# Attention backward for one query per head: K scores, dq and softmax sums ahead of the V transposes on TensorE, and the V load behind the dv stores

## The chip, the cores and the metric

One core of a Trainium2 chip. The metric is the device time of one execution in microseconds (us), median of several. Executions of one kernel are compared with executions of the kernel before on the same chip in the same rounds.

## The reference

32 heads, one query row, 8192 keys, head size 128, everything bfloat16. The outputs are the attention result and the gradients of q, k and v.

```python
def _fwd_reference(q, k, v):
    scale = q.shape[-1] ** -0.5
    scores = jnp.einsum('bhqd,bhkd->bhqk', q, k) * scale
    attn = _softmax(scores, axis=-1)
    return jnp.einsum('bhqk,bhkd->bhqd', attn, v)
# reference: out, vjp = jax.vjp(_f, q, k, v); returns (out, dq, dk, dv)
```

Each head reads 2 MB of K and 2 MB of V and writes 2 MB of dk and 2 MB of dv: 268 MB in all, for very little arithmetic. dk is the outer product of ds and q, dv that of p and grad_out; ds needs p, the V scores (grad_out times V) and one scalar.

## The kernel before

K is transposed on VectorE (`k_blocks`), V on TensorE with ScalarE copying out (`v_transposes`), so that both can be contracted over the head size. All transfers are issued by SyncE, in program order (in the trace of the kernel before: dk at 311.09 us, K 313.23, dk 314.01, dv 317.78, V 320.21, dv 320.64); it is the order of the Python calls below that each engine follows. There are three K buffers, two V buffers, and two each for dk and dv. `outer` also issues the stores, 1 MB each.

```python
    for h in range(H + 1):
        p_ = h - 1
        if h < H:
            x = st[h] = {}
            for u in range(NCH):
                k_blocks(h, u)              # VectorE, needs K of head h
            v_transposes(h, 0)              # TensorE, needs V of head h
            v_transposes(h, 1)
            k_scores(h)
            v_scores(h, 0)
        if h > 0:
            ds_of(p_)
            outer(p_, "dk", 0)
        ...                                 # mask, swap, first half of dq, dk part, maximum
        if h > 0:
            dq_of(p_, 1)
        if 0 < h and h + 2 < H:
            load_k(h + 2)
        if h > 0:
            outer(p_, "dk", 2)
        ...                                 # exponentials, rows, sum
        v_transposes(h, 2)
        contract(Vt[h], x["p"], x["m"][:, 2:3])      # the p column sums
        nc.scalar.copy(o_all[:, h:h + 1], x["m"][:, 2:3])
        v_scores(h, 2)
        v_transposes(h, 3)
        ...                                 # scalar product of o and grad_out
        v_scores(h, 3)
        outer(h, "dv", 0)
        outer(h, "dv", 1)                   # stores the first half of dv
        if h + 2 < H:
            load_v(h + 2)
        outer(h, "dv", 2)
        outer(h, "dv", 3)                   # stores the second half
```

Of the kernel before, what the change touches and what calls it, by code (L numbers as in the profile page):

```python
# [24 lines left out]
def kernel(  # L25
# [13 lines left out]
    _, H, S, D = k.shape  # L39
# [23 lines left out]
    def rows_of(x, h, c, parts):  # L63
        L = NT // parts
        return x[0, h].rearrange("(p n) d -> p n d", p=P)[:, c * L:(c + 1) * L, :]

    def slots(X, c, parts):
        L = NT // parts
        return X[:, c * L:(c + 1) * L, :]

    def load_k(h):
        Kt[h] = kpool.tile([P, NT, D], BF16, tag="K", name="Kt")
        parts = NCH if h == 0 else 1
        for c in range(parts):
            nc.sync.dma_start(slots(Kt[h], c, parts), rows_of(k, h, c, parts))

    def load_v(h):
        Vt[h] = vpool.tile([P, NT, D], BF16, tag="V", name="Vt")
        parts = NCH if h in (0, H - 1) else 1
        for c in range(parts):  # L80
            nc.sync.dma_start(slots(Vt[h], c, parts), rows_of(v, h, c, parts))
# [46 lines left out]
    def k_blocks(h, u):  # L128


        if u == 0:
            XK[h] = ktpool.tile([P, CH, NB, NCH, QD], F32, tag="XK", name="XK_sb")
        nc.vector.transpose(XK[h][:, :, :, u, :],  # L133
                            slots(Kt[h], u, NCH).rearrange("p g d -> p (g d)").bitcast(F32).rearrange(
                                "p (g w j) -> p g w j", g=CH, w=NB))

    def k_scores(h):
        x = st[h]
        x["s"] = psS.tile([P, 512], F32, tag="s", name="s_ps")
        out = x["s"][:, 0:NT].rearrange("p (a g) -> p g a", a=NQ)  # L140
        cols = XK.pop(h).rearrange("p g w u i -> p (g w u i)").bitcast(BF16).rearrange(
            "p (g w ui e) -> p g w e ui", g=CH, w=NB, e=2)
        for g in range(CH):
            for c in range(2 * NB):
                nc.tensor.matmul(out[:, g, :], lhsT=cols[:, g, c // 2, c % 2], rhs=q_blk[:, h, c, :],  # L145
                                 start=(c == 0), stop=(c == 2 * NB - 1), skip_group_check=True)
# [18 lines left out]
    def v_transposes(h, c):  # L165
        T_ps = psT.tile([P, CH, P], BF16, tag="T", name="T_ps")
        for i in range(CH):
            nc.tensor.transpose(T_ps[:, i, :], Vt[h][:, c * CH + i, :], ident[:])  # L168
        X = tpool.tile([P, CH, P], BF16, tag="XT", name="XT_sb")
        nc.scalar.copy(X.rearrange("p c s -> p (c s)").bitcast(F32),  # L170
                       T_ps.rearrange("p c s -> p (c s)").bitcast(F32))
        XV[h, c] = X

    def v_scores(h, c):
        X = XV.pop((h, c))
        if c == 0:
            st[h]["dp"] = psD.tile([P, 512], F32, tag="dp", name="dp_ps")
        for i in range(CH):
            n = c * CH + i
            nc.tensor.matmul(st[h]["dp"][:, n:n + 1], lhsT=X[:, i, :], rhs=doT[:, h:h + 1],  # L180
                             start=True, stop=True, skip_group_check=True)

    def contract(Xt, rep, out_col, first=0, last=NT):
        for n in range(first, last):
            nc.tensor.matmul(out_col, lhsT=Xt[:, n, :], rhs=rep[:, n, 0:1],  # L185
                             start=(n == 0), stop=(n == NT - 1), skip_group_check=True)

    def outer(h, which, r):
        x = st[h]
        if r == 0:  # L190
            x[which] = gpool.tile([P, NT, D], BF16, tag=which, name="G_" + which)
        G, dst = x[which], out_2 if which == "dk" else out_3
        rep, row = x["ds"] if which == "dk" else x["p"], x["qd"][:, 0 if which == "dk" else 1, :]
        Q = NT // 4
        nc.vector.tensor_tensor(  # L195
            slots(G, r, 4).rearrange("p n (a b) -> p n a b", b=R),
            slots(rep, r, 4).unsqueeze(2).to_broadcast([P, Q, D // R, R]),
            row.rearrange("p (a b) -> p a b", b=R).unsqueeze(1).to_broadcast([P, Q, D // R, R]),
            op=ALU.mult)
        parts = 4 if h == H - 1 else NST  # L200
        if r % (4 // parts) == 4 // parts - 1:
            c = r // (4 // parts)
            nc.sync.dma_start(rows_of(dst, h, c, parts), slots(G, c, parts))

    def rows_bc(h):
        x = st[h]
        nc.tensor.matmul(x["m"][:, 256:512], lhsT=ident[0:H, h:h + 1].to_broadcast([H, P]),  # L207
                         rhs=rows[:].rearrange("h a d -> h (a d)"), start=True, stop=True,
                         skip_group_check=True)
        x["qd"] = small.tile([P, 2, D], BF16, tag="qd", name="qd")  # L210
        nc.scalar.copy(x["qd"][:].rearrange("p a d -> p (a d)"), x["m"][:, 256:512])
# [10 lines left out]
    def dq_of(h, half):  # L222
        out = st[h]["dp"][:, 128:129]
        contract(Kt[h], st[h]["ds"], out, half * NT // 2, (half + 1) * NT // 2)
        if half == 1:
            nc.scalar.copy(dq_all[:, h:h + 1], out)  # L226
# [4 lines that stand above are left out]
            x = st[h] = {}  # L231
            for u in range(NCH):
                k_blocks(h, u)
            v_transposes(h, 0)
            v_transposes(h, 1)
            k_scores(h)
            v_scores(h, 0)
        if h > 0:
            ds_of(p_)
            outer(p_, "dk", 0)  # L240
        if h < H:
            s_mask(h)
            s_swap(h)
        if h > 0:
            dq_of(p_, 0)
            outer(p_, "dk", 1)
        if h < H:
            mx = small.tile([P, 1], F32, tag="mx")
            nc.vector.reduce_max(mx[:], x["sn"], axis=AX.X)  # L249
            diag = small.tile([P, P], F32, tag="diag")  # L250
            nc.vector.tensor_scalar(diag[:], ident_f[:], mx[:], scale, op0=ALU.mult, op1=ALU.mult)  # L251
            x["m"] = psM.tile([P, 512], F32, tag="m", name="m_ps")
            nc.tensor.matmul(x["m"][:, 128:256], lhsT=ones_f[:], rhs=diag[:], start=True, stop=True,  # L253
                             skip_group_check=True)
        if h > 0:
            dq_of(p_, 1)
        if 0 < h and h + 2 < H:
            load_k(h + 2)
        if h > 0:
            outer(p_, "dk", 2)  # L260
        if h == 0:
            load_k(2)
        if h < H:
            nbias = small.tile([P, 1], F32, tag="nbias")
            nc.vector.tensor_reduce(nbias[:], x["m"][:, 128:256], axis=AX.X, op=ALU.max, negate=True)
            e = small.tile([P, NT], F32, tag="e")
            rs = small.tile([P, 1], F32, tag="rs")
            nc.scalar.activation(e[:], x["sn"], ACT.Exp, bias=nbias[:], scale=scale, accum_out=rs[:])
            rows_bc(h)
            v_scores(h, 1)  # L270
            nc.tensor.matmul(x["m"][:, 0:1], lhsT=ones_f[:], rhs=rs[:], start=True, stop=True,  # L271
                             skip_group_check=True)
        if h > 0:
            outer(p_, "dk", 3)
        if h == H:
            break
        rinv = small.tile([P, 1], F32, tag="rinv")
        nc.vector.reciprocal(rinv[:], x["m"][:, 0:1])  # L278
        x["p"] = small.tile([P, NT, R], BF16, tag="prep", name="p_rep")
        nc.scalar.activation(x["p"][:], e[:].unsqueeze(2).to_broadcast([P, NT, R]), ACT.Copy, scale=rinv[:])  # L280
        x["p_s"] = small.tile([P, NT], F32, tag="p_s", name="p_s")
        nc.vector.tensor_scalar(x["p_s"][:], e[:], rinv[:], scale, op0=ALU.mult, op1=ALU.mult)
        v_transposes(h, 2)
        contract(Vt[h], x["p"], x["m"][:, 2:3])
        nc.scalar.copy(o_all[:, h:h + 1], x["m"][:, 2:3])
        v_scores(h, 2)
        v_transposes(h, 3)
        nc.tensor.matmul(x["m"][:, 1:2], lhsT=do_f[:, h:h + 1].to_broadcast([P, P]), rhs=o_all[:, h:h + 1],
                         start=True, stop=True, skip_group_check=True)
        v_scores(h, 3)  # L290
        outer(h, "dv", 0)
        outer(h, "dv", 1)
        if h + 2 < H:
            load_v(h + 2)
        outer(h, "dv", 2)
        outer(h, "dv", 3)

# [40 lines left out]
```

## Time and profile before

| | before |
|---|---|
| median of 4 executions (range) | 675.08 us (674.03 to 675.94) |
| the profiled execution | 681.02 us, span 679.2 us |
| TensorE, VectorE, ScalarE busy | 77%, 75%, 26% |
| DMA engines | busy almost from start to end, 397 GB/s on average |
| one head, first and second half of the run | 20.54 and 21.66 us |

Note that the profiled execution was 5.9 us longer than the median.

The timeline of one head (start, length, engine, line, tensors; the bracket is idle time and what ended it):

```profile
299.74 0.34 SPq L81 DMA_DIRECT2D Vt<-in_v_dram  x1
...
304.30 3.59 PE L168 MATMUL T_ps<-ident,Vt 128*128 128x128 bf16 x32 [2.90 <-DMA Vt<-in_v_dram]
...
311.09 0.33 SPq L203 DMA_DIRECT2D out_dram<-G_dk  x1
...
313.23 0.34 SPq L75 DMA_DIRECT2D Kt<-in_k_dram  x1
...
320.21 0.34 SPq L81 DMA_DIRECT2D Vt<-in_v_dram  x1
```

A V load is issued every 20.5 us at the end of a head; TensorE waits for an earlier one at the start of the next; the dk store and the K load go out 7 to 9 us later.

**The landing marks.** Every transfer leaves 16 landing marks in the trace (3344 marks for the 209 transfers of the kernel before). The page counts 16 DMA engines, and I read the marks as one of each. A consumer that waits goes on right after the last mark: in the kernel before TensorE begins the V transposes mostly 0.045 to 0.047 us after it. The **gap** is last minus first mark of one transfer: how far the slowest engine is behind the fastest. The **step** is the time from the last mark of one transfer to that of the next: how long the slowest engine took for it. The undisturbed steps are 4.88 us for a 2 MB load (the K loads of the kernel before, 4.84 to 4.90 from 60 to 650 us) and 2.45 us for a 1 MB store (the kernel with transfers alone, below, takes 19.54 us a head; less two loads that leaves 2.45 for each of four stores). The marks do not name the engines. That the last mark is always the same engine's is inferred from how smoothly it falls behind. The figures made from the marks depend a little on the stretch chosen: counts by some 10 matmuls a head, rates by some tenths of a nanosecond.

### The profile page before, as it was taken

How to read it: one execution, taken by the hardware profiler on the slowest of the kernel's cores; microseconds unless marked ns; L12 is line 12 of the kernel's file. 1: busy time of each engine (PE TensorE's matmuls, PEld its weight loads, DVE VectorE, ACT ScalarE, POOL GpSimd, SP SyncE). 2: the span in 40 equal slices, each digit the busy share in tenths (PEclk: the TensorE clock that was granted, in tenths of full speed). 3: DMA queues.
4: the chain of work that ended last, by engine and by line, in shares of the span. 5: the costliest groups of instructions: out<-in, count | busy, mean ns of one | idle time of the engine just before them, and what ended most of it. 6: DMA issues, size and time to landing. Idle time of an engine off the chain costs nothing.

```text
span 679.2 us, 23039 instructions
## 1 busy us (share of the span) xinstructions
PE 524.0 (77%) x10727; PEld 497.6 (73%) x10727; DVE 508.7 (75%) x658; ACT 175.8 (26%) x321; POOL 0.7 (0%) x6
## 2 busy tenths in 40 slices
PE   3899887977778877778867787667967687676991
PEld 3888887877777877778867687666857687666891
DVE  4899888767797777797766966778667876769683
ACT  1333322322323222323222232122222232222330
POOL 0000000000000000000000000000000000000000
PEclk9555556566556666556655565655566556655665
DMA  8999999999999999999999999999999999999874
GB/s 335 421 415 422 427 419 424 425 424 419 414 425 425 429 424 425 426 425 421 417 413 392 391 390 415 388 378 379 404 385 394 393 383 413 391 397 376 353 319 182
DMA packets 29807, 269.94 MB, mean 397 GB/s; under 512 B 3472, under 2 KB 3472, under 8 KB 6032
## 3 DMA queue, kind: packets, MB, share of 16 engines
q1 hardware_dynamic: 29712, 268.48, 97.2%
q8 instruction: 83, 1.36, 0.7%
q14 instruction: 12, 0.10, 0.0%
HBM read 134.23 MB, written 134.23 MB: 395 GB/s over the span
## 4 chain that ended last, share of the span: by engine, by line
DMA 51%; PE 39%; DVE 7%; ACT 1%; issue 1%; SPq 0%
DMA Vt<-in_v_dram 50%; PE T_ps L168 20%; PE m_ps L185 5%; PE s_ps L145 5%; DVE G_dk L195 4%; PE dp_ps L180 3%; PE dp_ps L185 2%; PE m_ps L253 2%; PE m_ps L271 2%; DVE sm L151 1%; PE m_ps L207 1%; ACT XT_sb L170 1%; DVE diag L251 1%; DMA Kt<-in_k_dram 1%; DVE mx L249 0%
## 5 line engine op out<-in xcount | busy, mean ns | idle before, releaser
L168 PE MATMUL T_ps<-ident,Vt 128*128 128x128 bf16 x2048 | 233.6, 311 | 90.4 <-DMA Vt<-in_v_dram 88.8
L168 PEld LDWEIGHTS <-Vt 128*128 128x128 bf16 x2048 | 216.2, 149 | 93.0 <-DMA Vt<-in_v_dram 92.7
L170 ACT COPY XT_sb<-T_ps 128x1024 f32<-128x1024 f32 x128 | 129.6, 1012 | 298.7 <-PE T_ps L168 298.7
L195 DVE TENSOR_TENSOR G_dk<-ds_rep,qd 128x2048 bf16<-128x2048 bf16 x128 | 155.8, 1219 | 1.1
L195 DVE TENSOR_TENSOR G_dv<-p_rep,qd 128x2048 bf16<-128x2048 bf16 x128 | 148.3, 1221 | 9.1 <-ACT p_rep L280 8.5
L133 DVE STREAM_TRANSPOSE XK_sb<-Kt 128x1024 f32<-128x1024 f32 x128 | 148.1, 1213 | 2.6 <-DMA Kt<-in_k_dram 2.5
L151 DVE TENSOR_TENSOR sm<-s_ps,in_quad 128x256 f32<-128x256 f32 x32 | 13.6, 425 | 112.8 <-PE s_ps L145 112.8
L180 PE MATMUL dp_ps<-doT,XT_sb 128*128 128x1 bf16 x2048 | 73.6, 165 | 26.1 <-ACT XT_sb L170 25.0
L180 PEld LDWEIGHTS <-XT_sb 128*128 128x128 bf16 x2048 | 64.1, 103 | 36.7 <-ACT XT_sb L170 27.6
L185 PEld LDWEIGHTS <-Kt 128*128 128x128 bf16 x2048 | 63.6, 102 | 6.9 <-issue 2.9
L185 PE MATMUL dp_ps<-ds_rep,Kt 128*128 128x1 bf16 x2048 | 64.5, 165 | 1.4 <-issue 0.9
L185 PEld LDWEIGHTS <-Vt 128*128 128x128 bf16 x2048 | 61.1, 105 | 0.0
L185 PE MATMUL m_ps<-p_rep,Vt 128*128 128x1 bf16 x2048 | 60.5, 166 | 0.0
L145 PEld LDWEIGHTS <-XK_sb 128*128 128x128 bf16 x2048 | 58.5, 101 | 0.0
L145 PE MATMUL s_ps<-q_blk,XK_sb 128*128 128x4 bf16 x2048 | 58.3, 167 | 0.0
L226 ACT COPY dq_all<-dp_ps 128x1 f32<-128x1 f32 x32 | 5.1, 159 | 136.6 <-PE dp_ps L185 136.6
L253 PE MATMUL m_ps<-diag,ones_f 128*128 128x128 f32 x64 | 24.7, 488 | 11.0 <-DVE diag L251 11.0
L253 PEld LDWEIGHTS m_ps<-diag,ones_f 128*128 128x128 f32 x64 | 15.4, 300 | 13.9 <-DVE diag L251 13.9
L280 ACT ACTIVATE p_rep<-e,rinv 128x256 bf16<-128x256 f32 x32 | 16.3, 508 | 29.2 <-DVE rinv L278 29.2
L278 DVE RECIPROCAL rinv<-m_ps 128x1 f32<-128x1 f32 x32 | 5.4, 168 | 23.6 <-PE m_ps L271 23.6
L218 DVE SCALAR_TENSOR_TENSOR ds_rep<-dp_ps,pdt,p_s 128x256 bf16<-128x256 f32 x32 | 15.5, 484 | 4.4 <-PE dp_ps L180 1.1
L271 PE MATMUL m_ps<-rs,ones_f 128*128 128x1 f32 x64 | 18.5, 358 | 0.2 <-issue 0.2
(40 smaller groups left out, 162.1 us busy)
## 6 DMA issues: line engine op xcount, KB each, us to landing
Kt<-in_k_dram SPq DMA_DIRECT2D x31, 2048.0 KB, 21.9
out_dram<-G_dv SPq DMA_DIRECT2D x62, 1024.0 KB, 23.9
out_dram<-G_dk SPq DMA_DIRECT2D x62, 1024.0 KB, 20.2
Vt<-in_v_dram SPq DMA_DIRECT2D x30, 2048.0 KB, 25.4
Vt<-in_v_dram SPq DMA_DIRECT2D x8, 512.0 KB, 13.9
Kt<-in_k_dram SPq DMA_DIRECT2D x4, 512.0 KB, 5.3
out_dram<-G_dv SPq DMA_DIRECT2D x4, 512.0 KB, 11.5
out_dram<-G_dk SPq DMA_DIRECT2D x4, 512.0 KB, 9.4
```

Source lines behind the costliest of these rows:

```text
L133: nc.vector.transpose(XK[h][:, :, :, u, :], slots(Kt[h], u, NCH).rearrange("p g d -> p (g d)").bitcast(F32).rearrange("p (g w j) -> p g w ...
L145: nc.tensor.matmul(out[:, g, :], lhsT=cols[:, g, c // 2, c % 2], rhs=q_blk[:, h, c, :], start=(c == 0), stop=(c == 2 * NB - 1), skip_group ...
L151: nc.vector.tensor_tensor(x["sm"][:], x["s"][:, 0:NT].rearrange("p (a g) -> p a g", a=NQ).unsqueeze(2) .to_broadcast([P, NQ, NCH, CH]), in ...
L168: nc.tensor.transpose(T_ps[:, i, :], Vt[h][:, c * CH + i, :], ident[:])
L170: nc.scalar.copy(X.rearrange("p c s -> p (c s)").bitcast(F32), T_ps.rearrange("p c s -> p (c s)").bitcast(F32))
L180: nc.tensor.matmul(st[h]["dp"][:, n:n + 1], lhsT=X[:, i, :], rhs=doT[:, h:h + 1], start=True, stop=True, skip_group_check=True)
L185: nc.tensor.matmul(out_col, lhsT=Xt[:, n, :], rhs=rep[:, n, 0:1], start=(n == 0), stop=(n == NT - 1), skip_group_check=True)
L195: nc.vector.tensor_tensor(slots(G, r, 4).rearrange("p n (a b) -> p n a b", b=R), slots(rep, r, 4).unsqueeze(2).to_broadcast([P, Q, D // R, ...
L218: nc.vector.scalar_tensor_tensor(out=x["ds"][:], in0=x["dp"][:, 0:NT].unsqueeze(2).to_broadcast([P, NT, R]), scalar=pdt[:], in1=x["p_s"][: ...
L253: nc.tensor.matmul(x["m"][:, 128:256], lhsT=ones_f[:], rhs=diag[:], start=True, stop=True, skip_group_check=True)
L271: nc.tensor.matmul(x["m"][:, 0:1], lhsT=ones_f[:], rhs=rs[:], start=True, stop=True, skip_group_check=True)
L280: nc.scalar.activation(x["p"][:], e[:].unsqueeze(2).to_broadcast([P, NT, R]), ACT.Copy, scale=rinv[:])
```

## The change

The intent: V is needed only in the middle of a head, so that the K side of a head can run while V is still on its way. No operation is added or removed. The V load moves in SyncE's order from between the two dv stores to behind both.

```diff
             for u in range(NCH):
                 k_blocks(h, u)
-            v_transposes(h, 0)
-            v_transposes(h, 1)
             k_scores(h)
-            v_scores(h, 0)
+            if 0 < h < H - 1:
+                load_v(h + 1)
         if h > 0:
             ds_of(p_)
             outer(p_, "dk", 0)
+            dq_of(p_, 0)
         if h < H:
             s_mask(h)
             s_swap(h)
         if h > 0:
-            dq_of(p_, 0)
+            dq_of(p_, 1)
             outer(p_, "dk", 1)
+        if 0 < h and h + 2 < H:
+            load_k(h + 2)
...                                  (second half of dq, load_k and v_scores(h, 1) cut from their old places, rows_bc moved up)
-        v_transposes(h, 2)
+        v_transposes(h, 0)
         contract(Vt[h], x["p"], x["m"][:, 2:3])
         nc.scalar.copy(o_all[:, h:h + 1], x["m"][:, 2:3])
-        v_scores(h, 2)
-        v_transposes(h, 3)
+        v_transposes(h, 1)
         nc.tensor.matmul(x["m"][:, 1:2], ...)
+        v_scores(h, 0)
+        v_transposes(h, 2)
+        v_scores(h, 1)
+        v_transposes(h, 3)
+        v_scores(h, 2)
         v_scores(h, 3)
         outer(h, "dv", 0)
         outer(h, "dv", 1)
-        if h + 2 < H:
-            load_v(h + 2)
```

More of the change, by code (lines that the diff above doesn't have):

```diff
@@ L254 @@
                              skip_group_check=True)
-        if h > 0:
-            dq_of(p_, 1)
-        if 0 < h and h + 2 < H:
-            load_k(h + 2)
+            rows_bc(h)
         if h > 0:
@@ L268 @@
             nc.scalar.activation(e[:], x["sn"], ACT.Exp, bias=nbias[:], scale=scale, accum_out=rs[:])
-            rows_bc(h)
-            v_scores(h, 1)
             nc.tensor.matmul(x["m"][:, 0:1], lhsT=ones_f[:], rhs=rs[:], start=True, stop=True,
```

## The prediction

> **What bounds the kernel now.** I read the page first: busy shares, the slices and the two DMA lines.
>
> ```profile
> PE 524.0 (77%) x10727; PEld 497.6 (73%) x10727; DVE 508.7 (75%) x658; ACT 175.8 (26%) x321; POOL 0.7 (0%) x6
> DMA  8999999999999999999999999999999999999874
> GB/s 335 421 415 422 427 419 424 425 424 419 414 425 425 429 424 425 426 425 421 417 413 392 391 390 415 388 378 379 404 385 394 393 383 413 391 397 376 353 319 182
> q1 hardware_dynamic: 29712, 268.48, 97.2%
> q8 instruction: 83, 1.36, 0.7%
> L168 PE MATMUL T_ps<-ident,Vt 128*128 128x128 bf16 x2048 | 233.6, 311 | 90.4 <-DMA Vt<-in_v_dram 88.8
> ```
>
> No compute engine is full; the DMA engines are, from the second slice to the 37th. But the rate falls from about 424 to about 390 GB/s in the middle of the run while the busy share stays at 9, and TensorE waits 88.8 us for V. The chain of waits in order of time gives the pace:
>
> ```profile
> 160.55 3.60 PE T_ps L168 x32
> ...
> 324.84 3.58 PE T_ps L168 x32
> ...
> 600.51 27.59 DMA Vt<-in_v_dram
> 628.15 3.59 PE T_ps L168 x32
> ...
> 645.75 3.44 PE T_ps L168 x32
> ```
>
> Each line is the start of a head whose V has just landed. 160.55 to 324.84 is 8 heads, 20.54 us each; 324.84 to 628.15 is 14 heads, 21.66 us each. Head 30, which waits for nothing more, takes 645.75 - 628.15 = 17.6 us, so compute has 3 to 4 us to spare in every head.
>
> Why 27.6 us for a 2 MB load, when the engines move 2 MB in 5 us? The landing records hold the answer: each transfer leaves 16 marks, one for each DMA engine. At 30 us the first and last mark of a transfer are 2 us apart, at 162 us 6 us, at 327 us 14 us; from there the gap stays between 14 and 17 us. So **one engine falls steadily behind** (the records do not name it; I take it to be the same one). The first marks advance by 19.54 us a head, the last by 20.54. The last marks of successive transfers follow each other without a gap up to 677 us, the end of the run. The kernel is bound by its slowest DMA engine, from about 118 us on, to the end.
>
> The likely cause is the 83 packets of queue q8. [...] That is 2.6 packets a head; at the 1.0 us a head lost, 0.4 us each. The change adds and removes no matmul, so this load stays.
>
> From about 340 us on the last mark of a V load takes 5.6 to 6.3 us after the one before it, where it took 4.88. That is the step from 20.54 to 21.66. It begins just when the first marks show gaps, that is when the fast engines have eaten their lead and run dry in each head. That the one causes the other is my choice: the same heads also read addresses beyond the first half of K and V, and the trace of one kernel cannot separate the two.
>
> [...]
>
> **The change part by part.** No instruction is added or removed; only orders change. The durations are those of one head in the timeline.
>
> The path on TensorE, from the start of a head's K scores: scores 1.79, the new ds meanwhile on VectorE (ds 0.48, dk part 1.22, mask 0.42: 2.25 us). First half of dq 0.96, swap 0.32: 3.05. Max on VectorE, after a dk part, and diag: 4.1. Max broadcast 0.80: 4.9. nbias after the next dk part: 5.65. Exp 0.52: 6.3. Sum 0.59: **6.9 us**; only here is V needed. Then four transpose groups at 1.73 (6.9), column sums 1.69, the o product 0.53, four V-score groups at 0.59 (2.4), and one exposed ScalarE copy before the last group (0.85): 12.3. A head is 19.2 us (estimate) in place of 17.6, since V transposes no longer fill the softmax waits. In the middle that lies beside the transfers: 19.2 is under 20.5. VectorE needs some 16 us a head.
>
> V loads: the buffer now comes free at 6.9 + 4 x 1.73 + 1.69 + 0.53 + 2 x 0.59 = 17.2 us into head h, and is needed 6.9 us into head h+2. With a period P the load has 2P - 10.3, about 30.8 us. Before, it was issued at 299.74 and needed two heads later at 340.8 less the head's own 15.9 us: 2P - 15.9 = 25.1, and exactly that is the landing time of 25.1 us. So V may arrive **5.7 us later**. K is issued earlier in its head and keeps a margin like the present one (29 us against a landing of 21.9).
>
> What is that worth? Not 5.7 us a head, as the slow engine is never idle. It buys queue depth, a longer lead for the fast engines before they run dry. Before: SyncE holds back the next dk store, eighth in line, until V lands:
>
> ```profile
> SPq L203 <- DMA Vt<-in_v_dram: 96.6, 27, 5.3
> Vt<-in_v_dram SPq DMA_DIRECT2D x30, 2048.0 KB, 25.4
> Kt<-in_k_dram SPq DMA_DIRECT2D x31, 2048.0 KB, 21.9
> ```
>
> At V's landing seven transfers, 9 MB, lie on the slow engine: at 2.47 us a MB 22.2 us. The next is issued 6.8 us later (304.3 to 311.09): room for a lead of 15.4 us, as seen (14 to 17). After: at V's landing dk, K, dk, dv, dv, V and the next dk are queued, again 9 MB, but the next K load stands ready and goes out at once: a lead of about 22 us. The lead grows 1.0 us a head, so the fast engines run dry 6.8 heads later; each of these heads costs 20.54 in place of 21.66: **6.8 x 1.12 = 7.6 us**.
>
> Start and tail: head 0 frees V some 2 us later, with 30 us of transfers queued, so no DMA engine stops. At the end two heads are 1.6 us slower each, and V's 7 us later need pays for it. The slow engine has about 25 us of writes after the last V load, against some 16 us of compute left: it still ends last. Both: 0.
>
> **The rivals.** First: nothing, as the engine's bytes and refills are the same. For it speaks the unbroken row of last marks, and that the slow V reads might come from the addresses; then 675 us. Second: the slow V reads go altogether, since they meet other transfers in the new order, or come earlier. At most 14 heads x 1.12 = 16 us: 660. Third: TensorE becomes the bound. At 19.2 us it is 1.3 under the DMA pace; should the waits come out 2 us longer, a head takes 21.2, on all 32 heads some 680. Against it: 1.79 + 0.96 + 0.32 + 1.04 + 0.80 + 0.39 + 0.59 = 5.9 us of work in the 6.9 leaves little to go wrong. Fourth, a naive reading: the 88.8 us of waits for V disappear. They cannot, as the transfers fill the time.
>
> **Range and chances.** 675.6 - 7.6 = 668.0. The rivals give 660, 675 and 680; I take 657 to 677. Over 2% faster means below 662.1, which needs most of the second rival: 0.18. Slower by 2% is above 689: 0.02. Within: 0.80.
>
> **What would show it.** In the changed trace: TensorE's wait for V stays, but before the first transposes of a head in mid-head, with V landing 28 to 32 us after issue; the gap between first and last mark grows to over 20 us; the drop from 424 to 390 GB/s comes some 7 heads later, near 480 us; the last marks stay unbroken to the end; a head without waits takes 19.2 us. If the drop comes at 340 us again, the addresses are its cause and my gain is wrong. If the last marks show gaps, compute has become the bound.

Its durations are those of the trace, in which the granted clock of TensorE was 0.57 on average. Its 2.47 us a MB is 1024 KB at the 424 GB/s of the page (estimate); the last marks give 20.54 / 8 = 2.57. That each of the 16 marks is one engine's is its reading. "Refills" are the packets of queue q8, which the page labels "instruction" (83 of 16 KB); their number follows that of the instructions (53 in after_thin, which has 7808 matmuls and weight loads fewer).

## More of the kernel before

In the table of windows (from:to, length, then busy us and number of instructions of TensorE, its weight loads, VectorE, ScalarE and GpSimd, the granted clock of TensorE, DMA share, GB/s) of the kernel before:

```profile
300.00:320.00 20.00, 15.82 (x335) 15.08 (x334) 15.32 (x21) 5.19 (x10) 0.00 (x0) 0.59 1.01 424
400.00:420.00 20.00, 14.99 (x316) 14.41 (x313) 14.83 (x20) 4.72 (x6) 0.00 (x0) 0.50 1.00 393
500.00:520.00 20.00, 15.18 (x326) 14.33 (x325) 14.53 (x19) 5.45 (x10) 0.00 (x0) 0.59 0.98 386
```

The DMA share is 0.98 to 1.01 in all three, yet 424 GB/s are moved in the first, and 393 and 386 in the later ones: this share does not tell the rate.

## The result, and the profile after

| | before | after |
|---|---|---|
| median of 4 (range) | 675.08 us (674.03 to 675.94) | 668.05 us (667.11 to 668.76) |
| ratio | | 0.9896 (95% interval 0.9875 to 0.9916) |
| profiled execution | 681.02 us | 668.76 us |

The ratio is the mean time of one kernel's runs over that of the other's of the same rounds, so not quite the ratio of the medians. The change is worth 7.0 us or 1.0%: clear of noise. A second set of runs on another chip gave 668.36 against 674.06 us, ratio 0.9901.

The same page lines of the changed kernel: DMA share, rate in 40 slices, instruction packets, and the first V transposes with the idle time before them.

```profile
DMA  8999999999999999999999999999999999999783
GB/s 330 414 425 424 419 427 414 424 423 426 425 425 424 425 425 424 425 429 423 423 427 426 423 416 422 413 412 418 395 423 418 397 416 406 409 420 403 270 357 142
q8 instruction: 83, 1.36, 0.7%
L168 PE MATMUL T_ps<-ident,Vt 128*128 128x128 bf16 x2048 | 228.7, 302 | 31.9 <-DMA Vt<-in_v_dram 31.9
```

The rate holds at some 424 GB/s to the 23rd slice (before: to the 20th) and then falls to about 412, not to 390. TensorE's wait for V falls from 88.8 to 31.9 us. The table of windows says the same:

```profile
300.00:320.00 20.00, 16.56 (x335) 15.54 (x335) 15.45 (x19) 5.65 (x10) 0.00 (x0) 0.50 1.00 423
400.00:420.00 20.00, 15.08 (x329) 14.10 (x327) 15.34 (x20) 5.09 (x11) 0.00 (x0) 0.57 1.01 416
500.00:520.00 20.00, 14.58 (x333) 13.59 (x334) 15.92 (x20) 5.48 (x10) 0.00 (x0) 0.67 1.01 419
```

Where did the waits go? First the waits of SyncE in the changed kernel (waiter, what it waited for, us in total, times, longest), then the landing times:

```profile
SPq L203 <- DMA out_dram<-G_dk: 111.7, 52, 2.5
SPq L203 <- DMA Kt<-in_k_dram: 110.8, 26, 5.2
SPq L75 <- DMA Vt<-in_v_dram: 97.5, 23, 4.5
```

```profile
Kt<-in_k_dram SPq DMA_DIRECT2D x31, 2048.0 KB, 28.0
out_dram<-G_dv SPq DMA_DIRECT2D x62, 1024.0 KB, 25.8
out_dram<-G_dk SPq DMA_DIRECT2D x62, 1024.0 KB, 28.0
Vt<-in_v_dram SPq DMA_DIRECT2D x30, 2048.0 KB, 28.3
```

SyncE now waits before nearly every issue for an older transfer to land; each transfer uses one of eight completion semaphores in turn (all 209 in both traces), and never are more than eight in flight: eight, the new one included, at 164 of the 209 issues, where it was 69 before. A K load waits for V, as predicted. All four kinds of transfer now take 26 to 28 us to land, where K took 21.9 and dk 20.2 before: the queue is full. The chain that ended last is accordingly a chain of transfers:

```profile
238.86 28.31 DMA Vt<-in_v_dram
267.24 27.99 DMA Kt<-in_k_dram
295.29 25.81 DMA out_dram<-G_dv
321.16 28.92 DMA Vt<-in_v_dram
```

Each was released by the landing of the one above it; four heads pass from one V to the next of the chain (321.16 - 238.86 = 82.3 us, 20.6 a head).

The landing marks, gap in us at about the same times, and pace of the last mark:

| | before | after |
|---|---|---|
| gap near 160, 241, 324 us | 5.9, 9.9, 13.9 | 7.6, 11.8, 15.9 |
| gap near 406, 489, 572 us | 16.0, 16.9, 16.6 | 20.6, 21.5, 21.9 |
| first marks begin to show idle time | about 320 to 335 us | about 390 to 405 us |
| pace of the last mark while the gap grows | 20.5 us a head | 20.6 us a head |
| pace afterwards | 21.7 us a head | 20.7 us a head |
| **slow loads**: steps of 2 MB loads less 4.88 us, with their signs, summed from the third such load on | 17.4 us | 3.3 us |
| last mark of the run | 678.3 us | 666.1 us |

The steps follow each other without a hole to the end in both (last mark at 678.3 of 679.2 us and at 666.1 of 667.0): the slowest DMA engine sets the time in both. So the 12.2 us between these two traces must lie in its steps. The slow loads give 17.4 - 3.3 = 14.1 us; the 124 stores of 1 MB give back 1.9 us (334.0 us in all, against 332.1 before). That is the whole of it.

The profiled execution of the kernel before was one of its slower ones. Other executions of kernels with the old order that ran in 675 to 677 us show 11 to 13 us of slow loads (below). With these the same sum gives 6 to 8 us (estimate), which fits the 7.0 us between the medians.

### The profile page after: what moved, and what is told of

Its sections match the earlier page's. It is cut to its first block, busy times and chain, and to the rows that moved or that the text cites. A ratio compares the mean times of both kernels' runs of the same rounds, so it can differ in the third digit from the quotient of the medians.

```text
span 667.0 us, 23105 instructions
## 1 busy us (share of the span) xinstructions
PE 516.8 (77%) x10727; PEld 485.8 (73%) x10727; DVE 512.5 (77%) x658; ACT 182.1 (27%) x321; POOL 0.7 (0%) x6
## 4 chain that ended last, share of the span: by engine, by line
DMA 75%; PE 17%; DVE 3%; ACT 2%; issue 1%; SPq 0%; ACTq 0%
DMA Kt<-in_k_dram 26%; DMA Vt<-in_v_dram 26%; DMA out_dram<-G_dv 23%; PE T_ps L168 7%; PE s_ps L145 2%; PE dp_ps L185 2%; PE m_ps L185 2%; PE dp_ps L180 1%; DVE XK_sb L133 1%; ACT XT_sb L170 1%; PE m_ps L255 1%; DVE G_dk L195 1%; PE m_ps L268 1%; PE s_ps L161 0%; ACT qd L211 0%
## 5 line engine op out<-in xcount | busy, mean ns | idle before, releaser
L168 PE MATMUL T_ps<-ident,Vt 128*128 128x128 bf16 x2048 | 228.7, 302 | 31.9 <-DMA Vt<-in_v_dram 31.9
L168 PEld LDWEIGHTS <-Vt 128*128 128x128 bf16 x2048 | 201.1, 142 | 33.8 <-DMA Vt<-in_v_dram 33.6
L180 PEld LDWEIGHTS <-XT_sb 128*128 128x128 bf16 x2048 | 74.7, 106 | 27.2 <-ACT XT_sb L170 27.2
L145 PE MATMUL s_ps<-q_blk,XK_sb 128*128 128x4 bf16 x2048 | 59.1, 168 | 23.2 <-DVE pdt L216 20.5
L145 PEld LDWEIGHTS <-XK_sb 128*128 128x128 bf16 x2048 | 56.5, 103 | 25.5 <-DVE pdt L216 22.3
L185 PEld LDWEIGHTS <-Kt 128*128 128x128 bf16 x2048 | 59.9, 104 | 12.3 <-issue 12.3
L185 PEld LDWEIGHTS <-Vt 128*128 128x128 bf16 x2048 | 61.1, 105 | 0.0
L268 PEld LDWEIGHTS m_ps<-rs,ones_f 128*128 128x128 f32 x64 | 16.0, 310 | 48.6 <-ACT e L267 48.6
L264 DVE TENSOR_REDUCE nbias<-m_ps 128x1 f32<-128x128 f32 x32 | 9.3, 292 | 22.0 <-ACT qd L211 22.0
L211 ACT CAST qd<-m_ps 128x256 bf16<-128x256 f32 x32 | 11.9, 372 | 42.4 <-PE m_ps L207 42.4
## 6 DMA issues: line engine op xcount, KB each, us to landing
Vt<-in_v_dram SPq DMA_DIRECT2D x30, 2048.0 KB, 28.3
out_dram<-G_dv SPq DMA_DIRECT2D x4, 512.0 KB, 16.9
```

The lines of the kernel that those rows point to most:

```text
L145: nc.tensor.matmul(out[:, g, :], lhsT=cols[:, g, c // 2, c % 2], rhs=q_blk[:, h, c, :], start=(c == 0), stop=(c == 2 * NB - 1), skip_group ...
L168: nc.tensor.transpose(T_ps[:, i, :], Vt[h][:, c * CH + i, :], ident[:])
L180: nc.tensor.matmul(st[h]["dp"][:, n:n + 1], lhsT=X[:, i, :], rhs=doT[:, h:h + 1], start=True, stop=True, skip_group_check=True)
L185: nc.tensor.matmul(out_col, lhsT=Xt[:, n, :], rhs=rep[:, n, 0:1], start=(n == 0), stop=(n == NT - 1), skip_group_check=True)
L211: nc.scalar.copy(x["qd"][:].rearrange("p a d -> p (a d)"), x["m"][:, 256:512])
L268: nc.tensor.matmul(x["m"][:, 0:1], lhsT=ones_f[:], rhs=rs[:], start=True, stop=True, skip_group_check=True)
```

## The experiments

Theory: the slowest DMA engine bounds the kernel. It is slowed further in the second half, when the queue is too short for its lag and the fast engines run dry. The change lets V land later, so the queue is longer. Rivals: the order of TensorE's work matters in itself; the place of the V load in the queue matters; the upper addresses are slow; and, for the lag itself, the instruction packets of queue q8 or something else.

All results are correct against the reference unless said otherwise. The table gives for each kernel the median, the gap at which it is capped, the lag of the slowest engine per head while the gap grows, the matmuls that TensorE begins during that engine's stores, per head, and the slow loads.

| kernel | us | gap cap, us | lag a head, us | matmuls in stores | slow loads, us |
|---|---|---|---|---|---|
| before | 675.1 | 15 to 17 | 1.00 | 204 | 17.4 |
| after | 668.1 | 21 to 22 | 1.04 | 226 | 3.3 |
| after_again | 668.4 | 21 to 22 | 1.04 | 226 | 4.6 |
| after_v_issue_old | 660.1 | 20 to 21 | 0.70 | 147 | 2.6 |
| before_v_issue_new | 678.1 | 12 to 14 | 0.95 | 191 | 11.1 |
| before_reverse | 678.5 | 15 to 17 | 1.00 | 202 | 12.9 |
| before_v3 | 672.3 | 14 to 16 | 1.00 | 206 | 8.4 |
| before_v3_ahead | 661.5 | 20 to 21 | 0.77 | 153 | 2.2 |
| after_thin | 655.0 | 20, at the end | 0.63 | 119 | 2.6 |
| before_thin | 661.8 | 14 to 16 | 0.75 | 139 | 11.2 |
| after_pool | 674.9 | 21 to 22 | 1.27 | 231 | 0.3 |
| dma_only | 637.3 | 3, does not grow | 0.00 | 0 | - |

The gaps, lags and slow loads are of one profiled execution each. Kernels that ran on different chips are better compared by their ratios to the before of the same rounds, which was 674.06 to 678.10 us. Up to about 4 us of the slow loads of any kernel lie in the first 150 us.

### Changed order on TensorE, V load at its old place

```diff
-            if 0 < h < H - 1:
-                load_v(h + 1)
...
         outer(h, "dv", 1)
+        if h + 2 < H:
+            load_v(h + 2)
         outer(h, "dv", 2)
```

> The changed kernel with the V load put back where it was issued before (between the second and third dv part). Theory, V is needed later on TensorE, which lets the lead of the fast DMA engines grow: the gain stays, 667 to 672 us, gap of first and last landing mark up to about 20 us. Rival, the gain comes from the new place of the V load in the queue: about 675 us, gap capped at 15 to 17 us.

Measured: **660.05 us** (660.00 to 660.23), ratio 0.9729 (0.9695 to 0.9764) against a before of 678.10 us on this chip. The rival is refuted: the gain does not come from the new place of the load. In the new order on TensorE that place even costs time: 8 us by the medians, which are of different chips, 11 us by the ratios (0.9896 against 0.9729). This was better than either theory expected, and the reason was not in my theory: the gap grows by 0.70 us a head in place of 1.04, with not one instruction fewer. Its rate in 40 slices:

```profile
GB/s 322 425 416 423 423 422 428 421 417 423 423 423 426 426 425 426 426 427 423 427 425 425 426 426 424 427 426 424 426 426 425 425 423 416 408 410 382 358 356 176
```

No fall before the 34th slice; the gap reaches 20 us only near 540 us.

### Order before, V load at its new place

```diff
             v_scores(h, 0)
+            if 0 < h < H - 1:
+                load_v(h + 1)
...
-        if h + 2 < H:
-            load_v(h + 2)
```

> The kernel before with only the V load moved to its new place, behind the dv stores. Theory: at V's landing one MB less is queued (8 MB in place of 9), so the gap is capped some 2.5 us lower, at 12 to 14 us, the fast engines run dry 2 to 3 heads earlier, and the time is 676 to 680 us. Rival, the queue order makes the gain: about 668 us.

Measured: 678.08 us (675.56 to 681.09), ratio 0.9997 (0.9954 to 1.0040): the same as before. It lies in the expected range only because the kernel before took 678.10 us on this chip; the expected loss of 1 to 5 us is not there. The gap is capped at 12 to 14 us as expected, and the first marks show idle time from 260 us on. But the kernel does not take longer for it, and between 260 and 340 us the last mark keeps its 20.5 us a head although the fast engines run dry. So running dry does not slow the slowest engine at once.

### Heads in reverse

```diff
-        return x[0, h].rearrange("(p n) d -> p n d", p=P)[:, c * L:(c + 1) * L, :]
+        return x[0, H - 1 - h].rearrange("(p n) d -> p n d", p=P)[:, c * L:(c + 1) * L, :]
...                                  (and the columns of q, grad_out, o and dq likewise)
```

> The kernel before with the heads taken in reverse order, so that the first 15 heads use the upper addresses. Theory, slow V reads start when the fast engines run dry: they start again near 340 us, and the time is 673 to 678 us. Rival, the upper addresses are slow: slow V steps (5.6 to 6.3 us on the last engine in place of 4.9) in the first half of the run, none after some 350 us.

Measured: 678.52 us (675.94 to 682.52), ratio 1.0007 (0.9955 to 1.0059). Slow loads start between 300 and 350 us again, with the lower half of the addresses now. The addresses are not the cause. (The time is 0.5 us above the expected range, as the kernel before took 678.10 us here.)

### Fewer matmuls

```diff
     def contract(Xt, rep, out_col, first=0, last=NT):
-        for n in range(first, last):
+        for n in (first, last - 1):
```

The columns in between are left out of dq and of the output; buffers, waits and transfers are as before. Its output is wrong, which doesn't matter for the time.

> The changed kernel with dq and the p column sums cut to their ends: 122 matmuls and 122 weight loads a head less, 244 of 717 instructions; dq and the output are wrong on purpose. Recorded theory, instruction refills slow the slowest DMA engine: a packet a head less at 0.4 us, so its lag grows 0.6 us a head in place of 1.0, and the time falls by 10 us or more, to 658 or less. Rival, after looking at all 16 marks: the refills hit some eight other engines in steps of 1.4 us, the slowest lags smoothly for another reason: its lag still grows 1.0 us a head and the time is 666 to 669 us.

Measured: 654.99 us (654.96 to 655.31); the before of these rounds took 678.10 us. The lag is 0.63 us a head: what the theory of the instruction packets expected, to the digit (53 packets in queue q8 in place of 83). Still these packets are not the reason. Looking at all 16 marks of the changed kernel near 308 us, relative to the first: five engines lie within 0.3 us, one at 1.2, one at 2.6, seven at 7.1 to 7.6, one at 9.6, and the last at 15.9. Followed through the run, the middle group moves in jumps of some 1.4 us, all about equally often. I read these as the 83 packets of queue q8 falling on some eight engines in turn: 39 of them had begun by 308 us, and the lags of the eight marks before the last then add up to 62 us, 1.6 us a packet (estimate). The last one shows no jump of that size. It loses a little in every store and nothing in any load, apart from three single steps of 0.5 to 0.7 us near 123, 342 and 565 us, beside three of the 8 KB instruction packets of another queue (q14, at 120.1, 340.1 and 560.5 us); most other kernels with compute show the like.

So I counted, for each step of the last mark in the stage where the gap grows, the matmuls that TensorE began in it. In the changed kernel the four stores of one head, with 48, 39, 101 and 48 matmuls, took 0.21, 0.15, 0.49 and 0.14 us more than 2.45; its two loads, with 17 and 82, took 0.00 and 0.02 us more than 4.88. A line through zero for the stores of each kernel gives **4.5 to 5.0 ns for each matmul with its weight load** in nine kernels (with other stretches 4.2 to 5.4; some 3.5 in before_thin, and 5.5 to 5.9 in after_pool, which has other instructions besides; both are described below); loads give less than 0.03 us on average, with up to 153 matmuls in one.

This also explains the 660 us: in that kernel one load coincides with some 120 matmuls that cost nothing, and the stores see 147 a head in place of 226. 79 x 4.7 ns is 0.37 us a head, and (1.04 - 0.70) x 32 = 11 us; measured 8 by the medians, 11 by the ratios. And it explains why after_thin is faster: 107 fewer, 0.50 us a head by the rule, 0.41 measured.

### The changed kernel again, and a third V buffer that is not used earlier

> The changed kernel itself once more, beside the others on this chip. Both theories: 666 to 670 us, gap of first and last mark capped at 21 to 22 us.

Measured: 668.36 us, as above. For the third V buffer only the constant `V_BUFS = 2` became 3 in the kernel before.

> The kernel before with a third V buffer, TensorE's order untouched. Theory, the length of the queue decides: V can be issued a head earlier, the eight transfers in flight become the only limit, the gap may grow beyond 17 us, and the time falls to 660 to 670 us, as with the change. Rival, the order of work on TensorE itself decides (less time lost in its waits): the time stays at 673 to 680 us.

Measured: 672.32 us (671.49 to 673.65), ratio 0.9966 (0.9946 to 0.9986), between the two expected ranges. The gap stays at 14 to 16 us. The experiment was badly aimed: SyncE issues in program order, as in the trace above, and the V load still stood behind the first dv store and was still asked for two heads ahead, so the buffer that came free was not used. It shows that the memory alone is worth some 2 us.

### Third V buffer, used: V three heads ahead

```diff
-V_BUFS = 2
+V_BUFS = 3
...
             load_k(2)
+            load_v(2)
...
-        if h + 2 < H:
-            load_v(h + 2)
+        if h + 3 < H:
+            load_v(h + 3)
```

> The kernel before, TensorE's order untouched, with a third V buffer and each V loaded three heads ahead in place of two, so that V is never late. Theory, the change gains because V may land later and the queue stays deeper: here K becomes the load that heads wait for, the gap of first and last mark is capped at 19 to 21 us in place of 15 to 17, the slow stage starts 3 to 5 heads later, 666 to 672 us. Rival, the order on TensorE itself matters: gap 15 to 17 us as before, 671 to 676 us.

Measured: **661.47 us** (661.17 to 661.52), ratio 0.9797 (0.9780 to 0.9813). TensorE's order is that of the kernel before, instruction for instruction, and still the gap grows to 20 to 21 us and the slow loads go. The waits of this kernel, in total, times and longest:

```profile
DVE XK_sb L133 <- DMA Kt<-in_k_dram: 76.8, 27, 3.4
PE T_ps L168 <- DMA Vt<-in_v_dram: 1.1, 1, 1.1
```

VectorE waits for K; TensorE waits for V only once. So V's later deadline alone is enough for the larger gap and for the slow loads to go; the new order of the work on TensorE is not needed for it. The time is below both expected ranges because the lag, at 0.77 us a head, fell as well, since here too the matmuls fall on other transfers (153 a head in stores). That part, (1.00 - 0.77) x 32 = 7 of the 13.6 us, is not due to the deadline as such.

### Only the transfers

K and V are loaded and stored back as dk and dv in the same pieces, four buffers each, no compute. Its output is wrong, which doesn't matter for the time.

> Only the transfers: K and V are loaded and stored back as dk and dv in the same pieces, no compute; results wrong on purpose. If the slowest engine's lag belongs to the transfers, the lag grows 0.7 to 1.0 us a head and the time is 650 to 662 us. If it comes from what the compute engines do (instructions and their refills), the 16 marks stay within 2 us and the time is 630 to 640 us, 32 heads at 19.54 us and some start.

Measured: 637.25 us (636.67 to 637.43). The 16 marks stay within 3.1 us from start to end (2 were expected), and the last one advances by 19.54 us a head. So the lag belongs to what the other engines do; without it the same transfers take 31 us less than the changed kernel. No run moved these bytes faster.

```profile
GB/s 316 423 428 426 420 430 413 434 428 424 433 425 431 429 427 433 427 430 432 426 431 429 427 433 428 428 432 427 431 429 427 432 427 429 433 426 431 425 427 329
q1 hardware_dynamic: 29136, 268.48, 99.9%
```

### Instructions on another engine

```diff
+            for _ in range(128):
+                nc.gpsimd.memset(tick[:], 0.0)
             k_scores(h)
```

> The changed kernel with 128 tiny writes a head on the idle GpSimd. The slowest engine's stores take 4.7 ns longer for each TensorE matmul (with its weight load) begun meanwhile. If it is any instruction that costs (2.4 ns each): about 64 of the 128 fall in stores, 0.15 us more lag a head, 5 us more: 672 to 675 us. If only TensorE's instructions count: lag 1.0 us a head as before, 666 to 670 us.

Measured: 674.87 us (674.26 to 675.26), ratio 0.9996 against before, 6.5 us more than the changed kernel in its second set of runs (668.36, on another chip). The lag rises from 1.04 to 1.27 us a head, by 0.23 (7 us on 32 heads). The added writes touch one element each and nothing waits for them:

```profile
L237 POOL MEMSET tick<- 1x1 f32 x4096 | 367.0, 90 | 236.1
```

So it is not TensorE as such: with GpSimd's instructions the slowest engine's stores take longer too (5.5 to 5.9 ns for each matmul begun in them, in place of 4.5 to 5.0). The other engines were not tried. How they do it these runs do not show, nor whether the recording of the trace has a part in it: for this kernel and the changed one the profiled execution is within 0.7 us of the next longest (675.26 against 675.03, 668.76 against 668.12), but the record has a span and a granted clock for every timed execution, so none of them may be free of recording. This stays open.

### Does the slow stage come with the gap or with the clock?

```diff
     def contract(Xt, rep, out_col, first=0, last=NT):          (in the kernel before)
-        for n in range(first, last):
+        for n in (first, last - 1):
```

> The kernel before with dq and the p column sums cut to their ends (122 matmuls a head less, wrong on purpose), TensorE's order as before. By 4.7 ns a matmul begun during stores, some 74 of the 122: lag 0.35 us a head less, 11 us in all; the gap then reaches 15 us at about 480 us in place of 340. Theory, slow loads come with the capped gap: none before 450 us, 4 us or less in all, time 655 to 660 us. Rival, they come at a time of the run (all kernels with the old order showed them from 345 us): they start at 345 us again, some 10 us in all, 661 to 666 us.

Measured: 661.83 us (657.25 to 663.14), ratio 0.9774 (0.9719 to 0.9829). Its output is wrong, which doesn't matter for the time. The gap reached 14 to 15 us near 440 to 480 us, and the first marks showed idle time from 400 us on. Slow loads: 0.0 us between 350 and 450 us, 1.5 us in the next 50, then 2.4, 2.1 and 1.0. So here they do not start at 345 us, but only when the gap has come to its cap. In before_v_issue_new, though, the gap is capped from 265 us on and the first slow load comes at 369 us: the cap alone does not bring them at once. The time alone would speak for the rival (661.83 lies in its range and 2 us above the theory's); it is when the slow loads start that decides. They add up to 7.0 us after 450 us where 4 were expected, and the lag fell by 0.25 us a head where 0.35 were expected.

The slow loads appear in five kernels, those capped at 12 to 17 us, and not in those capped at 20 us or more, though the fast engines of after, after_again and after_pool run dry for 250 us. Running dry is thus not enough. With a gap of 15 to 17 us the slowest engine's V load coincides with the K load of most others; with 21 us it coincides with stores of the middle group. That this is the reason is a reading of the marks, not shown: no run moved the one and kept the other.

The executions of a kernel also scatter more where slow loads appear: 5.9 us in before_thin and 6.6 us in before_reverse, at most 1.7 us in the kernels capped at 20 us or more.

### Two attempts to go further

First, taking load off the slowest engine: in every second head the last dv store cut into 120 and 8 partitions, on top of the fastest version.

```diff
+            if which == "dv" and c == 1 and h % SKIP == 0 and h < H - 1:
+                nc.sync.dma_start(rows_of(dst, h, c, parts)[0:120], slots(G, c, parts)[0:120])
+                nc.sync.dma_start(rows_of(dst, h, c, parts)[120:128], slots(G, c, parts)[120:128])
+            else:
                 nc.sync.dma_start(rows_of(dst, h, c, parts), slots(G, c, parts))
```

> The changed kernel with the V load at its old place, and in every second head the last dv store cut into 120 and 8 partitions, so that one engine (if its share goes by partition, the last) gets nothing of the 120. If that one is the slowest: its load falls by 1.2 us a head, more than it loses, the gap of the last mark grows no more beyond the others', and the time falls from 660 to 648 to 655 us. If it is another: 658 to 664 us.

Measured: 673.66 us (670.51 to 674.76), ratio 0.9975 against 0.9729 without the cut, and slower than both expected ranges. It was the wrong engine. The marks can be sorted here too: counted as 16 for a piece of 120 partitions and 9 for one of 8, they come out exactly on all eight semaphores, and one mark of each piece stands 0.5 us after its issue, long before the rest, so that 15 and 8 are left for the engines. Taken so, the last mark steps by 2.5 us in nearly every piece of 120, a full share, and by another 0.3 us in the piece of 8 that follows: the slowest engine has work in both. The additional transfer also uses up one of eight in flight; how much of the loss is due to that was not tested.

Second, fewer and larger stores: `NST = 2` became 1, on top of the fastest version.

> The fastest version so far (the changed order on TensorE, V load at its old place) with each gradient stored in one piece of 2 MB, so four transfers a head in place of six, and eight in flight are two heads. If the number in flight ends the growth of the gap: it grows beyond 21 us to the end, no dry engines, 655 to 659 us. If the later start of the stores costs more than that: 660 to 668 us.

Measured: **659.23 us** (658.39 to 659.60), ratio 0.9763 (0.9748 to 0.9778) against a before of 675.03 us. With four transfers a head in place of six the gap grows until about 600 us, to 22 us, and the fast engines hardly idle before that. Whether it is better than the version with 660.05 us is not shown: that ran on another chip, and its ratio (0.9729) is the lower one. Both beat the two kernels, as does the third version in bold.

## Why the prediction was right or wrong

The predicted time was 668.0 us, the measured 668.05. The mechanism held in outline, but the sum is closer than its terms deserve.

- **"The kernel is bound by its slowest DMA engine"**: right. The last marks have no hole in either kernel, and the transfers alone need 637 us.
- **"The likely cause is the 83 packets of queue q8"**: wrong. Some eight other engines move in steps of about 1.4 us, which I read as these packets; they are 7 to 10 us behind near 308 us, where the last one is 16. The slowest one loses 4.7 ns for each matmul begun during its stores. The arithmetic of 2.6 packets at 0.4 us fitted by chance, and so did after_thin. Only looking at all 16 marks, not at the first and the last, told the two apart.
- **V may arrive 5.7 us later, landing 28 to 32 us after issue**: right. V lands after 28.3 us, at the low end, and TensorE's wait for it remains, smaller, in mid-head.
- **"Room for a lead of about 22 us"**: right; the gap is capped at 21 to 22 us, and a K load waits for V's landing 23 times as described. before_v3_ahead shows that a later deadline for V is enough for a cap of 20 to 21 us.
- **"The fast engines run dry 6.8 heads later", near 480 us**: mis-sized. They run dry near 390 to 405 us, some three heads later. The gap was 2 us wider at equal times and grows 1.04 us a head, and the old cap lay nearer to 17 than to the 15.4 us that were worked out.
- **"Each of these heads costs 20.54 in place of 21.66", and the others still 21.66**: this is the step that failed. After the fast engines run dry a head costs 20.7 us, not 21.7. The slow loads do not come later, they hardly come at all (17.4 to 3.3 us). The second rival named this, with 16 us at most; it came true in part. Three heads at 1.12 us would be 3.4 us only; the other part of the gain is the cheaper late stage.
- **Why the sum fitted all the same**: this is luck. Two errors have opposite signs (the fast engines run dry three heads later and not 6.8; the heads after that cost 20.7 us and not 21.7), the profile of the kernel before was one of its slower executions, and the cost of the V load's new place, below, was left out. Between the two traces the gain is 12.2 us, between the medians 7.0.
- **A head without waits takes 19.2 us**: it takes 18.2 to 19.1, and the 19.1 include 2.0 us in which TensorE waits for nothing that the trace shows. In the chain of the changed kernel, heads 1 to 3 at the start of the run:

```profile
37.04 1.73 PE T_ps L168 x16
...
56.15 1.73 PE T_ps L168 x16
...
74.39 1.73 PE T_ps L168 x16
```

  Compute stayed under the DMA pace, so the third rival (TensorE becomes the bound) did not come about.
- **What the prediction did not have**: the V load's new place. The prediction counts it in the queue and gives it no cost; with the new order on TensorE it costs 8 to 11 us. The counts say how: with it 226 matmuls a head fall on the slowest engine's stores, without it 147. With the old order on TensorE the new place costs nothing measurable (ratio 0.9997). The rest of the change without it gained 18 us (678.10 to 660.05).

## What to carry to other kernels

When a DMA-bound kernel's transfers take several times longer to land than their bytes need (here 20 to 28 us, where 1 to 2 MB step by 2.45 to 4.88 us), look at the landing marks of all 16 engines: the pace may be that of one engine, and then the worth of a deadline moved later can be the depth of queue that it allows, not the wait that it removes. Count how many transfers may be in flight (here eight), and make a spare buffer useful by also asking for the data earlier in the issuing engine's order. A profile of one execution can overstate a gain (here 12.2 us against 7.0); check it against the spread of the timed ones before explaining every microsecond.
